# One budget per step for GpSimd's side work, and idle TensorE transposes in all odd steps ahead of the expert slots, in a kernel of top-k attention with a mixture of experts

## The chip, the cores and the metric

The kernel runs on one core of a Trainium2 chip. The metric is the device time of one execution in microseconds (us), the median of several runs. TensorE (PE) multiplies and transposes, VectorE (DVE), ScalarE (ACT) and GpSimd (POOL) work on tiles in SBUF, SyncE (SP) starts most of the transfers. Each engine takes its instructions in the order in which the program wrote them.

## What is computed

```python
scores = scale * np.matmul(q, k.transpose(0, 1, 3, 2))          # 8 batches, 8 heads, 576 x 576, head size 64
kth = np.partition(scores, -32, axis=-1)[..., -32:-31]          # the 32nd largest of each row
scores = np.where(scores >= kth, scores, -1e9)
attn = softmax(scores)                                          # over the row
x = (attn @ v).transpose(0, 2, 1, 3).reshape(4608, 512)
e_idx = np.argmax(x @ w_gate, axis=1)                           # one of 8 experts for each token
for e in range(8):
    mask = e_idx == e
    h = np.maximum(x[mask] @ w1[e], 0.0)                        # 512 -> 1024
    out[mask] = gate_w[mask, None] * eom[mask, e, None] * (h @ w2[e])
```

`gate_w` is the softmax probability of the chosen expert, `eom` a sigmoid of `x @ w_output_gate`. All is float32.

## The kernel before

**Steps.** The attention is cut into 36 tiles of 128 query rows and each tile into 4 head pairs, which gives 144 steps (`for i in range(NSTEP + 4)`, L959). A step writes the work of several head pairs at different stages: VectorE takes the eight largest of each eighth of a row one step ahead (`gmax`, L328) and ranks these candidates of pair i (`rank`, L330 to L339), ScalarE compares its scores with the 24th largest (`below`, L354), GpSimd adds the marks to the scores (`w<-s,marks`, L366, two operations of 128x576), VectorE takes the maxima of that (`window`, L383) and with them, one step later, the 32nd largest and the masked weights (`choose`, `weigh`, L412). TensorE turns the weights of pair i-2 (`flip`, L431: nine transposes in three parts, L438), multiplies those of pairs i-4 and i-3 with the values in every other step (`attend`, L472), and makes the scores of pair i+2 (`scores`, L301), which ScalarE copies (L309).

**Ahead of the slots.** In the first 32 steps (`LONE`, L814) one of the two heads is masked on ScalarE and GpSimd in place of VectorE (`veil`, `unveil`, L418 to L428), so that GpSimd has three 128x576 operations per step. In odd steps `flip` adds 12 transposes of the identity that nobody reads (`IDLE`, L441), but not in steps that carry a routing part (`extra`).

**Routing.** Every fourth step a tile of 128 tokens is done. Two routing parts follow in TensorE's order, `gates` (L502, L493) in an odd step and `rows` (L511, L493) in the next, both written into the same PSUM tile as part 1 of `flip` (`pst`). GpSimd scales the tile's rows in two operations (L515, kind "x") and SyncE writes them to DRAM (`x_rows`). The tiles are collected in 12 groups. After the last tile of a group, GpSimd scatters the tokens' numbers into expert lists (`ids`, L604 and L605, kind "ids") and, for 8 of the groups, computes a table of slots of up to 128 tokens of one expert (`slot_table`, L635: 32 small operations on one partition, kind "table").

**Slots.** From step 33 on a slot takes four steps: its list is loaded (`idt`, issued by ScalarE), GpSimd gathers its 128 rows (`fetch_x`, L754), TensorE turns them (`turn`, L764), multiplies with `w1` in two steps (L775) and with `w2` in two (L790), and GpSimd scatters the result (`put`, L800 and L801, kind "out"). 29 slots start beside the attention, the last in step 145; eleven run in a tail with no attention.

**Order of GpSimd's side work.** `later` puts an operation with an estimated cost into a list in order of due step. Three places in a step take from it: before `below`, kinds "ids" and "out" up to `DMAS` or `MORE`; after `veil`, kind "x" up to `SUMS`; near the step's end, kind "table" up to `TABLES`, in parts of four operations at 0.72. `fetch_x` comes last and its cost counts nowhere, since `spent` is set to zero at each place:

```python
spent[0] = 0.0
run_slow(SUMS, ("x",))
spent[0] = 0.0
...
spent[0] = 0.0
run_slow(TABLES, ("table",))
ahead("x", fetch_x, 2, "id", 1)
```

A group's slots are listed (`queue_slots`) when no "ids" and no "table" waits any more.

Of the kernel before, what the change touches and what calls it, by code (L numbers as in the profile page):

```python
# [10 lines left out]
F32 = mybir.dt.float32  # L11
# [10 lines left out]
ACT = mybir.EngineType.Activation  # L22

P = 128
# [6 lines left out]
USUAL = 9  # L31


SUMS = 1.3
DMAS = 2.2
TABLES = 2.4
MORE = 3.2

NLIST = 12

# [2 lines left out]
def tile_topk_attention_moe(  # L43
# [11 lines left out]
    nc = tc.nc  # L55
# [24 lines left out]
    NID = E * REG + MAXS * P  # L80
# [18 lines left out]
    FIXED = {}  # L99
# [99 lines left out]
    def run(exact, stack):  # L199
# [25 lines left out]
        def later(what, cost, f, due):  # L225
            queued[0] += 1
            slow.append((step[0] + due, queued[0], what, cost, f))
            slow.sort()
# [16 lines left out]
        def waiting(what):  # L245
            return any(x[2] == what for x in slow)
# [184 lines left out]
        def flip(i, part, extra=None, idle=0):  # L431

            pt = EP[i].rearrange("p a s -> p (a s)")
            c0, c1 = ((0, 4), (4, 5), (5, 9))[part]
            n = c1 - c0
            ps = ps_t.tile([P, 4, P], F32, name="pst")
            for c in range(c0, c1):
                nc.tensor.transpose(ps[:, c - c0, :], pt[:, c * P:(c + 1) * P], ident)  # L438
            ev = extra(ps) if extra else None
            for _ in range(idle):  # L440
                nc.tensor.transpose(ps[:, 3, :], ident, ident)  # L441
            x = wk.tile([P, n, P], F32, name=f"pT{n}", bufs=6 if n == 4 else 3)
            PTT.setdefault(i, []).append(x)
            if part == 2:
                del EP[i]

            def copies():
                nc.scalar.activation(x, ps[:, :n, :], AF.Copy)  # L448
                if ev:
                    ev()  # L450
            return copies
# [283 lines left out]
            W.setdefault(s, [None, None])[1] = b  # L735

        def fetch_id(s, g, k, rows):
            eng, queue = ACT, nc.scalar
            if g in FIXED:
                place = slice(FIXED[g][k] * REG, FIXED[g][k] * REG + P)  # L740
            else:
                ov = nc.values_load(SLOT[g][0:1, 1, k:k + 1], engines=[eng], min_val=0, max_val=NID - P,
                                    skip_runtime_bounds_check_because="expert regions and the spare one hold every slot")
                place = bass.ds(ov, P)
            it = mp.tile([P, 4], I32, name="idt", bufs=NLIST)
            queue.dma_start(it, ids[place, :])
            G[s] = [it]

        def fetch_x(s, g, k, rows):
# [171 lines left out]
        def route(g):  # L921
            ops = group_route(g, LGT[g])
            small.extend(ops[:-1])
            if g < NGRP - 1:
                def some(part):
                    for f in part:
                        f()
                if g in FIXED:
                    parts = [settle(FIXED[g])]
                else:  # L930
                    table = slot_table(g, False)
                    parts = [table[x:x + 4] for x in range(0, len(table), 4)]

                def tables():
                    for part in parts:
                        later("table", 0.18 * len(part), lambda part=part: some(part), 1)

                def chosen():
                    order.extend((g, k, (GROUPS[g][-1] + 1) * P) for k in range(EARLY[g]))
                if g in FIXED:  # L940
                    chosen()
                    small.extend([ops[-1], tables])
                else:
                    small.extend([tables, ops[-1], lambda: not waiting("table"), chosen])
                small.append(lambda: not waiting("ids"))
                small.append(lambda: not waiting("table"))
                small.append(lambda: queue_slots(g, EARLY[g], (GROUPS[g][-1] + 1) * P))
            else:
                small.extend(ops[-1:])
# [9 lines left out]
        for i in range(NSTEP + 4):  # L959
# [10 lines left out]
                fill(2)  # L970
                weigh(i - 1)
            spent[0] = 0.0
            run_slow(DMAS if i < LONE else MORE, ("ids", "out"))
            fetch_ids()
            if i < NSTEP:
                below(i)
# [4 lines left out]
            if 2 <= i < NSTEP + 2:  # L981
                early.append(flip(i - 2, 0))
                if i < LONE or not extra:
                    early.append(flip(i - 2, 1, extra, idle=0 if i >= LONE or extra or i % 2 == 0 else IDLE))
            if 4 <= i < LONE and i % 2 == 0:
                late.append(attend(i - 4))
            ahead_of_slot()
# [22 lines left out]
            if 1 <= i <= NSTEP:  # L1010
                veil(i - 1)
            spent[0] = 0.0
            run_slow(SUMS, ("x",))
            spent[0] = 0.0
            if i < NSTEP:
                exps(i)
            for f in late:
# [6 lines left out]
            if i < NSTEP:  # L1024
                window(i, 0)
                window(i, 1)
            spent[0] = 0.0
            run_slow(TABLES, ("table",))
            ahead("x", fetch_x, 2, "id", 1)
            side_use()  # L1030
            fill(3)
            if i < NSTEP:
# [26 lines left out]
        def background():  # L1059
            step[0] += 1  # L1060
            extra = side_start()
            if extra:
                extra(ps_t.tile([P, 4, P], F32, name="pst"))()
                side_use()
            fill(60)
            run_slow(1e9, ("table", "ids", "x", "out"))

        tail[0] = True
        HL = {}
# [149 lines left out]
```

## Time and profile before

| | |
|---|---|
| three runs | 1259.98, 1263.29, 1263.64 us; median 1263.29 |
| the profiled execution | 1265.04 us; its span 1263.3 us |
| busy in the span | TensorE 1163.9 us (92%), VectorE 1066.4 (84%), ScalarE 950.2 (75%), GpSimd 715.0 (57%) |
| chain that ended last | TensorE 38%, VectorE 23%, issue 16%, GpSimd 15%, ScalarE 5% |

The span is some 2 us shorter than the execution's time, because the execution also has a start and an end outside the instructions. A busy share is a mean over the whole span; the first 32 steps, the steps with slots and the tail have different limits and have to be read apart.

### The profile page before, as it was taken

The page shows a single profiled execution, that of the slowest core. Times are in us where ns is not written, and L with a number is a line of the kernel's source. Part 1 is how long each engine was busy: PE and PEld are TensorE (multiplying, and loading weights), DVE is VectorE, ACT ScalarE, POOL GpSimd, SP SyncE. Part 2 cuts the span into 40 slices and gives each one's busy share as a digit, 9 for nine tenths or more (in the row PEclk, how much of TensorE's full clock was granted, in tenths as well). Part 3 has the DMA queues.
Part 4 walks back from the last instruction along what each step waited for, and adds up shares of the span by engine and source line. Part 5 has one row for each costly group of instructions (what it writes and reads, how often), then busy time and mean ns, then how long its engine had stood idle before and what let it go on. Part 6 is the DMA issues. An engine that isn't in the chain of part 4 may idle for free.

```text
span 1263.3 us, 31073 instructions
## 1 busy us (share of the span) xinstructions
PE 1163.9 (92%) x9862; PEld 893.0 (71%) x9862; DVE 1066.4 (84%) x6145; ACT 950.2 (75%) x1892; POOL 715.0 (57%) x1191
## 2 busy tenths in 40 slices
PE   5777777899999999999999999999999999979996
PEld 3555555677777777777776777777777777869995
DVE  6999898899999999998998999989999988344442
ACT  5998898888878887787887878878787877334542
POOL 6666668554546584866566765576755485321110
PEclk7989898899999999999999999999999999989998
DMA  5300136067545448486554655566464444599980
GB/s 138 70 18 27 43 115 254 19 203 249 191 162 159 144 145 304 141 239 226 191 175 173 205 204 192 183 210 210 133 237 169 160 148 172 193 341 353 365 320 21
DMA packets 113734, 227.47 MB, mean 180 GB/s; under 512 B 19206, under 2 KB 37894, under 8 KB 112528
## 3 DMA queue, kind: packets, MB, share of 16 engines
q1 hardware_dynamic: 99712, 205.61, 48.4%
q0 software_dynamic: 7552, 18.96, 4.4%
q10 hardware_dynamic: 6288, 0.74, 0.5%
q8 instruction: 82, 1.34, 0.4%
q14 instruction: 100, 0.82, 0.2%
HBM read 206.68 MB, written 20.69 MB: 180 GB/s over the span
## 4 chain that ended last, share of the span: by engine, by line
PE 38%; DVE 23%; issue 16%; POOL 15%; ACT 5%; ACTq 1%; DMA 1%; POOLq 0%
PE pm L775 9%; PE pm L790 8%; PE po L472 7%; DVE cand L328 7%; PE ps L301 6%; POOL w L366 6%; PE pst L438 6%; DVE v L383 4%; DVE ep L412 4%; DVE cand L339 3%; DVE v L336 3%; POOL ids L605 2%; ACT marks L363 1%; POOL out_dram L801 1%; DVE x L394 1%
## 5 line engine op out<-in xcount | busy, mean ns | idle before, releaser
L366 POOL TENSOR_TENSOR w<-s,marks 128x576 f32<-128x576 f32 x288 | 363.3, 1283 | 256.6 <-DVE ep L412 121.2
L328 DVE MAX8 cand<-s 128x8 f32<-128x72 f32 x2304 | 323.9, 219 | 14.2 <-ACT s L309 14.2
L775 PE MATMUL pm<-xs,w1t 128*128 128x128 f32 x2560 | 297.3, 275 | 0.0
L775 PEld LDWEIGHTS pm<-xs,w1t 128*128 128x128 f32 x2560 | 292.0, 192 | 0.9
L438 PE MATMUL pst<-ident,ep 128*128 128x128 f32 x1296 | 221.7, 287 | 64.9 <-ACT ep L428 46.8
L363 ACT ACTIVATE marks<-s,v 128x576 int8<-128x576 f32 x288 | 220.6, 769 | 67.8 <-DVE v L336 44.9
L383 DVE MAX8 v<-w 128x8 f32<-128x576 f32 x288 | 207.8, 749 | 51.8 <-POOL w L366 51.6
L438 PEld LDWEIGHTS pst<-ident,ep 128*128 128x128 f32 x1296 | 147.9, 143 | 141.3 <-ACT ep L428 55.0
L448 ACT ACTIVATE pT<-pst 128x512 f32<-128x512 f32 (+1 forms) x432 | 200.5, 485 | 32.3 <-PE pst L493 26.9
L790 PE MATMUL pm<-w2t,ht 128*128 128x512 f32 x464 | 208.9, 593 | 0.0
L412 DVE SCALAR_TENSOR_TENSOR ep<-s,kth,ep 128x576 f32<-128x576 f32 x256 | 200.5, 816 | 0.0
L309 ACT ACTIVATE s<-ps 128x1152 f32<-128x1152 f32 (+1 forms) x145 | 163.3, 1127 | 43.2 <-PE ps L301 41.1
L378 ACT ACTIVATE ep<-s,v 128x576 f32<-128x576 f32 x256 | 185.7, 771 | 11.4 <-POOL v L352 11.4
L301 PE MATMUL ps<-kst,qst 64*128 64x288 f32 (+1 forms) x1280 | 184.8, 437 | 5.1 <-ACT s L309 5.1
L472 PEld LDWEIGHTS po<-pT,v 128*64 128x64 f32 x3200 | 168.2, 144 | 25.0 <-issue 24.0
L472 PE MATMUL po<-pT,v 128*64 128x128 f32 (+1 forms) x3200 | 185.3, 275 | 0.1
L790 PEld LDWEIGHTS pm<-w2t,ht 128*128 128x128 f32 x464 | 83.6, 190 | 83.7 <-issue 83.4
L301 PEld LDWEIGHTS ps<-kst,qst 64*128 64x128 f32 (+1 forms) x1280 | 99.5, 180 | 47.3 <-issue 23.8
L336 DVE MAX8 v<-cand 128x8 f32<-128x16 f32 (+2 forms) x864 | 128.7, 189 | 0.0
L801 POOL DMA_INDIRECT out_dram<-y,idt x40 | 48.1, 1203 | 134.4 <-ACT y L797 113.4
L339 DVE MATCH_REPLACE8 cand<-v,cand 128x16 f32<-128x16 f32 (+1 forms) x576 | 95.1, 174 | 0.0
L352 POOL TENSOR_SCALAR v<-v 128x2 f32<-128x2 f32 x144 | 37.1, 258 | 94.6 <-DVE v L336 93.9
(169 smaller groups left out, 1234.6 us busy)
## 6 DMA issues: line engine op xcount, KB each, us to landing
w1t<-in_w_dram SPq DMA_DIRECT2D x40, 2048.0 KB
w2t<-in_w_dram SPq DMA_DIRECT2D x40, 2048.0 KB
x_rows<-xu SPq DMA_DIRECT2D x36, 256.0 KB
qst<-in_qa_dram SPq DMA_DIRECT2D x70, 128.0 KB
v<-in_va_dram SPq DMA_DIRECT2D x8, 1024.0 KB
kst<-in_ka_dram SPq DMA_DIRECT2D x14, 576.0 KB
v<-in_va_dram SPq DMA_DIRECT2D x16, 64.0 KB
ids<-far SPq DMA_DIRECT2D x1, 678.0 KB
```

Source lines behind the costliest of these rows:

```text
L301: nc.tensor.matmul(ps[qs, a, n, :288], Q[t][rows, hp, qs], K[b][rows, hp, cols], start=True, stop=True)
L328: nc.vector.max(out=c[:, 8 * g:8 * g + 8], in_=SC[i, a][:, g * GW:(g + 1) * GW])
L363: nc.scalar.activation(m.bitcast(I8).rearrange("p (s b) -> p s b", b=2)[:, :, 1], s, AF.Sign, bias=vs[:, a, PIVOT - 1:PIVOT], scale=-(1.0 ...
L366: x = nc.gpsimd.tensor_tensor(w, s, m, op=ALU.add)
L378: nc.scalar.activation(EP[i][:, a, :], SC[i, a], AF.Exp, bias=VV[i][0][:, a, 32:33], scale=SCALE)
L383: nc.vector.max(out=VV[i][0][:, a, 24:32], in_=SW[i][0][a])
L412: LAST[0] = nc.vector.scalar_tensor_tensor(e, SC.pop((i, a)), kth_col(i, a), e, op0=ALU.is_ge, op1=ALU.mult, accum_out=SM[t][:, 2 * hp + a ...
L438: nc.tensor.transpose(ps[:, c - c0, :], pt[:, c * P:(c + 1) * P], ident)
L448: nc.scalar.activation(x, ps[:, :n, :], AF.Copy)
L472: nc.tensor.matmul(po[a * 64:(a + 1) * 64, k, qs], lhs, rhs, start=half and not k and not m, stop=(c == 3 and k == 1 and m == len(TT[t]) - 1))
L775: nc.tensor.matmul(ph[:, f - f0, :], w[:, c, f * P:(f + 1) * P], XS[s][:, c, :], start=(c == 0), stop=(c == NC - 1))
L790: nc.tensor.matmul(PY[s], HT[s][:, f, :], w[:, f, :], start=(f == 0), stop=(f == NF - 1))
```

## The change

The three places become two. Before `below` "ids" and "out" go as before, up to 2.6, but up to 1.4 (one of them) while a table waits. After `veil` the gathers go first, then "x", "table" and "done" in their order, all on one budget: 1.3 ahead of the slots, 2.75 with them. A table's operations are put into the list singly at 0.27, and the last six of its 32, which only the next table needs, are a kind of their own ("done") that listing the slots does not wait for. The idle transposes are written into a PSUM tile of their own (`spare`, of the experts' pool) and are no longer left out in steps with a routing part. One variable in `fetch_id` is renamed away.

```diff
--- before.py
+++ after.py
@@ -31,10 +31,10 @@
 USUAL = 9
 
 
-SUMS = 1.3
-DMAS = 2.2
-TABLES = 2.4
-MORE = 3.2
+DMAS = 2.6
+MORE = 1.4
+FEW = 1.3
+MANY = 2.75
 
 NLIST = 12
 
@@ -437,8 +437,9 @@
             for c in range(c0, c1):
                 nc.tensor.transpose(ps[:, c - c0, :], pt[:, c * P:(c + 1) * P], ident)
             ev = extra(ps) if extra else None
+            spare = pools["p"].tile([P, 4, P], F32, name="pm") if idle else None
             for _ in range(idle):
-                nc.tensor.transpose(ps[:, 3, :], ident, ident)
+                nc.tensor.transpose(spare[:, 0, :], ident, ident)
             x = wk.tile([P, n, P], F32, name=f"pT{n}", bufs=6 if n == 4 else 3)
             PTT.setdefault(i, []).append(x)
             if part == 2:
@@ -735,15 +736,14 @@
             W.setdefault(s, [None, None])[1] = b
 
         def fetch_id(s, g, k, rows):
-            eng, queue = ACT, nc.scalar
             if g in FIXED:
                 place = slice(FIXED[g][k] * REG, FIXED[g][k] * REG + P)
             else:
-                ov = nc.values_load(SLOT[g][0:1, 1, k:k + 1], engines=[eng], min_val=0, max_val=NID - P,
+                ov = nc.values_load(SLOT[g][0:1, 1, k:k + 1], engines=[ACT], min_val=0, max_val=NID - P,
                                     skip_runtime_bounds_check_because="expert regions and the spare one hold every slot")
                 place = bass.ds(ov, P)
             it = mp.tile([P, 4], I32, name="idt", bufs=NLIST)
-            queue.dma_start(it, ids[place, :])
+            nc.scalar.dma_start(it, ids[place, :])
             G[s] = [it]
 
         def fetch_x(s, g, k, rows):
@@ -922,18 +922,12 @@
             ops = group_route(g, LGT[g])
             small.extend(ops[:-1])
             if g < NGRP - 1:
-                def some(part):
-                    for f in part:
-                        f()
-                if g in FIXED:
-                    parts = [settle(FIXED[g])]
-                else:
-                    table = slot_table(g, False)
-                    parts = [table[x:x + 4] for x in range(0, len(table), 4)]
+                table = settle(FIXED[g]) if g in FIXED else slot_table(g, False)
+                aside = 0 if g in FIXED else 6
 
                 def tables():
-                    for part in parts:
-                        later("table", 0.18 * len(part), lambda part=part: some(part), 1)
+                    for n, f in enumerate(table):
+                        later("table" if n < len(table) - aside else "done", 0.27, f, 1)
 
                 def chosen():
                     order.extend((g, k, (GROUPS[g][-1] + 1) * P) for k in range(EARLY[g]))
@@ -970,7 +964,7 @@
                 fill(2)
                 weigh(i - 1)
             spent[0] = 0.0
-            run_slow(DMAS if i < LONE else MORE, ("ids", "out"))
+            run_slow(MORE if waiting("table") else DMAS, ("ids", "out"))
             fetch_ids()
             if i < NSTEP:
                 below(i)
@@ -981,7 +975,7 @@
             if 2 <= i < NSTEP + 2:
                 early.append(flip(i - 2, 0))
                 if i < LONE or not extra:
-                    early.append(flip(i - 2, 1, extra, idle=0 if i >= LONE or extra or i % 2 == 0 else IDLE))
+                    early.append(flip(i - 2, 1, extra, idle=0 if i >= LONE or i % 2 == 0 else IDLE))
             if 4 <= i < LONE and i % 2 == 0:
                 late.append(attend(i - 4))
             ahead_of_slot()
@@ -1010,8 +1004,8 @@
             if 1 <= i <= NSTEP:
                 veil(i - 1)
             spent[0] = 0.0
-            run_slow(SUMS, ("x",))
-            spent[0] = 0.0
+            ahead("x", fetch_x, 2, "id", 1)
+            run_slow(FEW if i < LONE else MANY, ("x", "table", "done"))
             if i < NSTEP:
                 exps(i)
             for f in late:
@@ -1024,9 +1018,6 @@
             if i < NSTEP:
                 window(i, 0)
                 window(i, 1)
-            spent[0] = 0.0
-            run_slow(TABLES, ("table",))
-            ahead("x", fetch_x, 2, "id", 1)
             side_use()
             fill(3)
             if i < NSTEP:
@@ -1063,7 +1054,7 @@
                 extra(ps_t.tile([P, 4, P], F32, name="pst"))()
                 side_use()
             fill(60)
-            run_slow(1e9, ("table", "ids", "x", "out"))
+            run_slow(1e9, ("table", "done", "ids", "x", "out"))
 
         tail[0] = True
         HL = {}
```

GpSimd's order in step 89 before, in the middle of a group's table (`v` and `near` are the step's first operations, `spacer` stands ahead of each scatter, `sl_` and `first_row` are the table's):

```order
L352 TENSOR_SCALAR v_10131<-v_10131 128x2
L400 COPY near<-v_10012 128x4
L604 MEMSET spacer 1x1
L605 DMA ids<-entry,posi 43392x4
L800 MEMSET spacer 1x1
L801 DMA out_dram<-y,idt 4608x512
L366 TENSOR_TENSOR w<-s,marks_80 128x576
L366 TENSOR_TENSOR w<-s,marks_81 128x576
L515 TENSOR_TENSOR xu<-xu,r 128x256 x2
L675 TENSOR_TENSOR sl_jump<-first_row 1x8
L676 TENSOR_SCALAR sl_jump<-sl_jump 1x8
L679 TENSOR_TENSOR sl_way<-sl_past,sl_jump 1x24
```

The same step after the change:

```order
L352 TENSOR_SCALAR v_10241<-v_10241 128x2
L400 COPY near<-v_10111 128x4
L605 MEMSET spacer 1x1
L606 DMA ids<-entry,posi 43392x4
L366 TENSOR_TENSOR w<-s,marks_80 128x576
L366 TENSOR_TENSOR w<-s,marks_81 128x576
L754 DMA xg_129<-x_rows,idt 128x512
L669 TENSOR_SCALAR first_row<-pad_d 1x8
L670 TENSOR_TENSOR first_row<-first_row,done 1x8
L676 TENSOR_TENSOR sl_jump<-first_row 1x8
L677 TENSOR_SCALAR sl_jump<-sl_jump 1x8
L680 TENSOR_TENSOR sl_way<-sl_past,sl_jump 1x24
```

The scatter of the result and the two scalings have left the step (they stand in step 91), the gather has come up from the step's end to behind the second `w`, and six of the table's operations follow it where twelve stood. Before, the table was written in steps 88, 89 and 90 as 12, 12 and 8 operations; now it is 10, 6, 10 and, in step 91, the last 6. The other seven tables are spread in the same way.

TensorE's order from the scores of step 6 into step 7 before (`xT` is the attention's result, `lt` the gates' logits; the five `pst<-ident,ep` are parts 0 and 1 of `flip`, the four its part 2):

```order
L301 MATMUL ps<-kst,qst 128x288 x4
L438 MATMUL pst<-ident,ep 128x128 x5
L502 MATMUL pst<-xT,wg 32x128 x4
L493 MATMUL pst<-ident,xT 128x128 x2
L438 MATMUL pst<-ident,ep 128x128 x4
```

And after the change:

```order
L301 MATMUL ps<-kst,qst 128x288 x4
L438 MATMUL pst<-ident,ep 128x128 x5
L503 MATMUL pst<-xT,wg 32x128 x4
L494 MATMUL pst<-ident,xT 128x128 x2
L442 MATMUL pm<-ident 128x128 x12
L438 MATMUL pst<-ident,ep 128x128 x4
```

The 12 idle transposes stand between the gates' products and the last part of `flip`, and write `pm`. This is so in steps 7, 11, 15, 19, 23, 27 and 31; the other odd steps had them already. The steps in which each slot's products start are the same before and after.

## Rows read from the trace of the kernel before

**Rows 1.** Busy time by stage: start:end, length, engines' busy us, granted clock, DMA share, GB/s.

```profile
0.00:237.20 237.20, 167.70 (x1443) 121.72 (x1445) 210.73 (x1348) 202.44 (x426) 157.30 (x232) 0.86 0.31 90
237.20:1069.40 832.20, 823.53 (x7201) 617.69 (x7200) 777.35 (x4691) 673.29 (x1383) 518.98 (x910) 1.00 0.56 187
1069.40:1263.30 193.90, 172.66 (x1221) 153.62 (x1220) 78.32 (x110) 74.47 (x85) 38.71 (x50) 0.95 0.72 259
```

**Rows 2.** VectorE's waits in the slots' stage: total us, times, longest us.

```profile
DVE v L383 <- POOL w L366: 38.7, 49, 2.3
```

**Rows 3.** TensorE's waits in the same stage.

```profile
PE pst L502 <- ACT xT L474: 4.9, 6, 1.4
PE pst L764 <- DMA xg<-x_rows,idt: 1.6, 1, 1.6
```

**Rows 4.** Windows of steps 45 to 48, 101 to 104, and 89, 90, 91.

```profile
327.10:356.50 29.40, 29.40 (x248) 22.14 (x247) 27.66 (x164) 24.20 (x50) 15.37 (x21) 1.00 0.50 173
756.90:784.50 27.60, 27.60 (x235) 20.98 (x234) 27.35 (x166) 22.89 (x48) 15.36 (x22) 1.00 0.55 191
656.10:666.00 9.90, 9.90 (x115) 8.78 (x112) 7.39 (x45) 7.81 (x15) 8.93 (x19) 1.00 0.67 239
666.00:675.60 9.60, 9.33 (x88) 7.39 (x88) 6.80 (x41) 5.76 (x12) 8.29 (x22) 1.00 0.71 254
675.60:682.40 6.80, 5.41 (x31) 2.74 (x30) 6.80 (x44) 4.69 (x13) 3.88 (x9) 1.00 0.21 68
```

**Rows 5.** GpSimd's timeline, steps 88 and 89: start us, us, instruction, idle before.

```profile
652.81 2.52 POOL L366 TENSOR_TENSOR w<-s,marks 128x576 f32<-128x576 f32 x2
655.29 0.20 POOL L652 TENSOR_TENSOR sl_cnt<-base,carry 1x8 f32<-1x8 f32 x1
...
658.53 0.60 POOL L669 TENSOR_TENSOR first_row<-first_row,done 1x8 f32<-1x8 f32 x1
...
660.24 1.09 POOL L605 DMA_INDIRECT ids<-entry,posi  x1 [0.17 <-issue]
...
665.11 1.21 POOL L515 TENSOR_TENSOR xu<-xu,r 128x256 f32<-128x256 f32 x2
...
670.81 1.13 POOL L754 DMA_INDIRECT xg<-x_rows,idt  x1 [0.61 <-DVE cand L328]
```

**Rows 6.** Windows of steps 5-6, 7, 10, 13, 20-21, 10-25, 31-32.

```profile
43.00:55.30 12.30, 9.15 (x89) 6.83 (x88) 12.13 (x80) 11.94 (x25) 8.16 (x11) 1.00 0.55 123
55.30:61.50 6.20, 3.86 (x26) 2.46 (x27) 6.17 (x43) 6.15 (x14) 4.11 (x6) 0.76 0.00 1
77.50:83.50 6.00, 4.60 (x57) 3.43 (x54) 5.96 (x40) 5.82 (x13) 4.03 (x6) 1.00 0.01 1
95.90:104.30 8.40, 6.64 (x51) 4.66 (x47) 6.84 (x43) 7.10 (x15) 5.21 (x8) 0.99 0.20 63
143.20:159.30 16.10, 13.41 (x138) 10.08 (x135) 13.04 (x82) 12.87 (x28) 9.27 (x13) 0.77 0.36 86
77.50:186.30 108.80, 80.45 (x807) 58.98 (x804) 101.11 (x644) 99.12 (x213) 69.89 (x89) 0.91 0.15 42
222.60:237.20 14.60, 9.48 (x53) 5.91 (x53) 13.46 (x90) 13.42 (x29) 10.49 (x14) 0.73 0.12 29
```

**Rows 7.** TensorE's timeline, steps 5, 10, 11 and 12.

```profile
45.24 1.47 PE L441 MATMUL pst<-ident 128*128 128x128 f32 x12
...
79.39 2.40 PE L472 MATMUL po<-pT,v 128*64 128x128 f32 x40
...
87.53 0.66 PE L438 MATMUL pst<-ident,ep 128*128 128x128 f32 x4 [0.94 <-ACT pT L448]
...
92.31 4.07 PE L472 MATMUL po<-pT,v 128*64 128x128 f32 x40
```

**Rows 8.** VectorE's timeline, end of step 12 and start of 13: reading the gates.

```profile
95.79 0.27 DVE L528 TENSOR_TENSOR tl<-pst,r 128x128 f32<-128x128 f32 x1
96.10 0.37 DVE L530 TENSOR_REDUCE lg<-tl 128x16 f32<-128x128 f32 x1
```

## Prediction

> **What bounds the kernel now.** I read the windows of the three stages first, then who waits in each, then single steps.
>
> By stage [rows 1] the first 32 steps take 237.2 us, the 112 steps with slots 832.2 us, the tail 193.9 us. The reader is to see that different engines are full: ahead of the slots VectorE (210.7 of 237.2) and ScalarE (202.4), TensorE with 167.7 at a mean granted clock of 0.86; in the slots' stage TensorE, 823.5 of 832.2, at full clock. The change touches nothing in the tail, and each slot starts in the same step as before, so the tail is costed at nothing; what covers it is its own weights' transfers (DMA share 0.72).
>
> *Slots' stage.* VectorE waits 38.7 us there for GpSimd's `w` [rows 2], and this is the number one would like to win. TensorE's own waits are the counter-check: 4.9 and 1.6 us [rows 3], together with smaller ones 832.2 - 823.5 = 8.7 us in which it is not busy. Steps 45 to 48 take 29.4 us with TensorE busy through all of them and GpSimd busy for 15.4; steps 101 to 104, with GpSimd no busier, take 27.6 [rows 4]. The difference is backlog. In steps 89 and 90 GpSimd is the last one (8.9 of 9.9 us, 8.3 of 9.6, where a step otherwise takes about 7, by 27.6 or 29.4 for four), and TensorE still works on through 9.9 of 9.9 and 9.3 of 9.6: it uses the stall to finish what lay before it. Only step 91, where it has caught up, shows it idle, 6.8 - 5.4 = 1.4 us. After such a stall VectorE sets a pace of 27.6 per four steps until TensorE is behind again, then TensorE sets 29.4. So over a cycle TensorE bounds this stage, and a GpSimd stall costs only what TensorE idles after it.
>
> *Ahead of the slots.* Step 10 takes 6.0 us at clock 1.00, step 13 takes 8.4, steps 20 and 21 together 16.1 at a mean clock of 0.77 [rows 6]. In step 12, at the lower of the two levels (1.2 GHz in place of 2.4), the 40 products of `attend` took 4.07 us, against 2.40 in step 10 [rows 7]; the scores behind them came late, then ScalarE's copy and marks, GpSimd's `w`, and with them VectorE in step 13. What TensorE did before a fall: steps 5 and 6, of which 5 has idle transposes, run at 1.00; step 7, an odd step without them, is at 0.76 over its length and the fall lies in it [rows 6]. There are eight such falls, the first in step 7 and the last in step 31 (both windows in [rows 6]): four in odd steps with a routing part and no idle transposes (7, 19, 27, 31), four in even steps (12, 16, 24, 30), none in an odd step with them.
>
> **The change part by part.**
>
> 1. *Idle transposes in steps 7, 11, 15, 19, 23, 27, 31.* Each adds 12 transposes, 1.47 us in step 5. They stand where TensorE waits 0.94 us for ScalarE in step 11 [rows 7], so at most 1.47 - 0.94 = 0.53 us per step goes behind the wait, and the scores come that much later. The lower bound of their cost is nothing (ScalarE is still at other work when the scores are done), the upper 7 x 0.53 = 3.7 us; I take 0.2 each, 1.4 in all. If the cover were gone, all 1.47 would count, 10.3 us. What they may give: undisturbed, a cycle of four steps takes 4 x 6.1 us (6.0 in step 10, 6.2 in step 7 [rows 6]), and the step after `rows` some 0.65 more, in which VectorE reads the gates (0.27 and 0.37 [rows 8]): 25.05. Steps 10 to 25 took 108.8 [rows 6], which is 108.8 - 4 x 25.05 = 8.6 us above it. The fall in step 7 resembles that in 19: steps 20 and 21 together take 16.1 against 6.1 + 6.75, so 3.2 more. Steps 31 and 32 take 14.6, but with VectorE busy for 13.5 of them [rows 6], so I count 1.0 there. Upper bound 8.6 + 3.2 + 1.0 = 12.8 us. The lower bound is no gain. The falls in even steps stand open: three of them (12, 16, 24) cost about 8.4 - 6.75 = 1.65 each, and no idle transposes are written into even steps. But those in the odd step before push the scores and the next transposes by up to 0.53 us into the gap in which the fall came. I take half of these 4.9 as won: 12.8 - 2.4 - 1.4 = **9.0 us**.
>
> 2. *GpSimd's budget.* No work is removed: scatters (pitch about 1.4 us with the memset ahead), gathers (1.13), scalings (1.21 for two) and table operations, 11 from 655.29 to 658.53, 0.30 us each [rows 5]. It is dealt out anew. Step 88 gets one scatter, `w` (2.52), 0.44 for the two small copies and 10 table operations: 1.4 + 2.52 + 0.44 + 3.0 = 7.4. Step 89: one scatter, the gather with its gap of some 0.3, six operations: 1.4 + 2.96 + 1.4 + 1.8 = 7.6. Step 90 is as 88, step 91 has scalings, scatter and the last six: 1.2 + 1.4 + 2.96 + 1.8 = 7.4. The sum is 29.8 us over four steps, beside TensorE's 29.4: GpSimd is then just level with TensorE in place of 9.9 and 9.6 us in two steps and idle around them. What is late next is TensorE, at its own pace. So the gain is bounded by its 8.7 idle us; the lower bound is nothing, since with 29.8 against 29.4 GpSimd may still be last at some steps. I take 6.0, nearer the upper end, because a lag of 0.4 us per group is small beside a backlog that lasted from step 91 to step 104. "ids" and "out" are delayed by a step or two at most; what waits for them (listing, list loads on ScalarE, turning the rows) has spare steps, since slots start as before.
>
> 3. *Moved without price:* the gather ahead of the scalings (its list was loaded at the step's start, and `w` runs for 2.52 us in between); idle transposes into another PSUM tile, which is free until step 33; the last six table operations, which only the next table reads; the budget 1.3 ahead of the slots, which still takes two scalings.
>
> **Sum.** 9.0 + 6.0 = 15.0 us. Against the profiled execution, 1265.0 - 15.0 = 1250.0; this execution lies 1.7 us above the median of the three runs, so I put the new median at 1263.3 - 15.0 = **1248.3 us**. A measurement of this kernel tells about 0.3% (3.8 us) from no change.
>
> **The rivals.**
>
> *VectorE's waits come back whole.* Were VectorE the bound of the slots' stage, 38.7 us [rows 2] would go and the time would be about 1225. Against it speaks TensorE, busy through the stalls. Chance 0.03.
>
> *Only one half works.* If the clock still falls in the even steps, or falls in others because the steps have moved against the times at which the clock changes, 3 us remain of part 1: 1263.3 - 9 = 1254. If GpSimd, full for four steps in place of two, leaves TensorE idle as before, part 2 is nothing: also 1254. Against the first: even steps without a routing part, such as step 10 at 1.00 [rows 6], never fell. Chance of one or the other 0.28.
>
> *Neither works, or one is eaten up,* 1260 to 1266: 0.09. That the change does not do what it says is excluded by the order: the transposes and the dealt-out table stand there.
>
> *Slower: the idle transposes do not hold the clock and are in the way.* TensorE has no slack in the first stage if the scores' end is what ScalarE waits for. Then each of the seven steps is 1.47 us longer, 10.3 us, while falls come as before: 1263.3 + 10.3 - 6.0 = 1267.6. It decides from the point where the scores end later than ScalarE's work before their copy. For it: ScalarE is busy in 202.4 of 237.2 us [rows 1], so any delay of it is passed on. Against it: odd steps with the transposes take 12.3 us together with the even step after them [rows 6], no more than two even steps. Chance 0.06. The Trainium skill (TensorE: Matmul & The Clock Gate, Part 4: PE-mode transpose) says that full clock "doesn't engage for transpose-mode (it doesn't count as PE-busy the same way)". By that rule the new transposes could hold nothing and this rival would be the forecast, 1267.6. The trace speaks against it: steps 5 and 6 hold 1.00 with them, step 7 falls without them.
>
> **How the numbers follow.** Both halves work: 0.54, with 1240 to 1254 as its own range (both upper bounds, 12.8 + 8.7 = 21.5 us, and the 1.7 us by which executions differ; 9 us at the least). One half: 0.28. VectorE's waits: 0.03. Neither: 0.09. Slower: 0.06. The range from 1240 to 1260 leaves out the last, the first rival and most of "neither". Faster than 1259.5 is 0.54 + 0.28 + 0.03 and a little of "neither", 0.86; within 0.3% 0.08; slower 0.06.
>
> **What would show it.** Steps 8, 9, 13, 17, 20 and 21 at 6 to 7 us, the granted clock of the first stage above 0.95 (0.86 now), 12 transposes in step 11 with little or no wait behind them. In the slots' stage: steps 89 and 90 at 7 to 8 us, VectorE's wait for `w` well under 38.7, but TensorE's busy time unchanged near 823 and the stage shorter only by TensorE's idle time. The forecast is wrong if the stage shrinks by much more than 8.7 us (then TensorE was not its bound), or if falls of the clock remain in even steps, or if the steps with idle transposes are longer than their neighbours.

## The result, and the profile after

The changed kernel takes 1244.24 us in the median of four runs (1243.55 to 1246.53), the kernel before 1261.65 beside it (1259.98 to 1263.64): a ratio of 0.9865, 95% interval 0.9841 to 0.9888, 17.4 us faster. The forecast was 1248.3 in a range from 1240 to 1260. The profiled execution took 1243.92, its span 1242.1.

The same three stages after the change (start:end, length, busy us of PE, PEld, DVE, ACT, POOL with the number of instructions, granted clock, DMA share, GB/s), to be held against [rows 1]:

```profile
0.00:226.10 226.10, 161.00 (x1529) 120.14 (x1531) 209.59 (x1348) 201.31 (x427) 156.97 (x232) 0.93 0.33 95
226.10:1050.30 824.20, 820.71 (x7200) 617.00 (x7196) 785.22 (x4691) 672.52 (x1382) 512.56 (x910) 1.00 0.56 189
1050.30:1242.10 191.80, 171.94 (x1221) 153.15 (x1221) 77.65 (x110) 74.56 (x85) 38.51 (x50) 0.96 0.72 262
```

The first stage is 237.2 - 226.1 = 11.1 us shorter at a clock of 0.93 in place of 0.86, the slots' stage 832.2 - 824.2 = 8.0, the tail 193.9 - 191.8 = 2.1. These add to 21.2, more than the medians' 17.4, since the profiled execution of before lies 3.4 us above its median (1265.04 against 1261.65).

**Ahead of the slots**, windows of steps 7, 10, 13, 20 with 21, 10 to 25, 31 with 32 [rows 6]:

```profile
54.90:61.10 6.20, 4.80 (x43) 3.60 (x42) 6.17 (x43) 6.12 (x14) 4.10 (x6) 1.00 0.00 1
74.00:80.10 6.10, 4.70 (x57) 3.52 (x56) 6.07 (x42) 5.85 (x13) 4.12 (x6) 1.00 0.01 1
92.40:99.10 6.70, 4.95 (x38) 3.44 (x35) 6.62 (x43) 6.38 (x14) 5.18 (x8) 1.00 0.25 80
136.50:149.50 13.00, 9.61 (x133) 7.37 (x130) 12.72 (x81) 12.53 (x28) 9.27 (x13) 1.00 0.25 68
74.00:175.30 101.30, 76.20 (x855) 56.69 (x853) 100.27 (x646) 98.67 (x213) 69.95 (x89) 1.00 0.15 41
211.70:226.10 14.40, 9.46 (x65) 6.78 (x66) 13.44 (x90) 13.60 (x30) 10.48 (x14) 0.85 0.13 30
```

Step 13 takes 6.7 us in place of 8.4, steps 20 and 21 13.0 in place of 16.1, and the 16 steps from 10 to 25 take 101.3 in place of 108.8. From step 7 to 25 the clock stays at the upper level; three falls are left, in steps 26, 30 and 32. (The granted clock of 0.93 also holds the stretch of 17.1 us at the lower level that stands at the execution's start, as in the kernel before.) TensorE's timeline in step 11, where the new transposes stand [rows 7]:

```profile
82.67 0.44 PE L494 MATMUL pst<-ident,xT 128*128 128x128 f32 x2
82.95 1.47 PE L442 MATMUL pm<-ident 128*128 128x128 f32 x12
84.26 0.60 PE L438 MATMUL pst<-ident,ep 128*128 128x128 f32 x4
84.79 1.24 PE L301 MATMUL ps<-kst,qst 64*128 64x288 f32 x8
```

The wait of 0.94 us is gone and the idle transposes take its place; the last part of `flip` follows without a gap. Counted from the step's start the scores come 4.7 us into it, 0.1 later than before.

**With slots**, first VectorE's wait for GpSimd and TensorE's own waits [rows 2, 3]:

```profile
DVE v L383 <- POOL w L366: 23.0, 41, 1.8
```

```profile
PE pst L503 <- ACT xT L475: 1.4, 2, 0.8
PE pst L764 <- DMA xg<-x_rows,idt: 0.9, 1, 0.9
PE pst L438 <- ACT pT L449: 0.6, 1, 0.6
```

then the windows of steps 45 to 48, 101 to 104, and 89, 90, 91 [rows 4]:

```profile
315.90:345.30 29.40, 29.40 (x249) 22.14 (x247) 27.81 (x165) 24.20 (x50) 14.81 (x21) 1.00 0.50 174
733.00:760.60 27.60, 27.60 (x225) 20.77 (x223) 27.55 (x165) 22.95 (x48) 14.82 (x21) 1.00 0.49 179
642.10:650.00 7.90, 7.90 (x97) 7.39 (x97) 7.27 (x43) 6.26 (x14) 7.04 (x14) 1.00 0.68 252
650.00:658.30 8.30, 8.30 (x95) 7.12 (x89) 6.93 (x43) 7.19 (x13) 7.60 (x18) 1.00 0.12 34
658.30:666.50 8.20, 7.57 (x51) 4.12 (x45) 8.10 (x44) 4.27 (x12) 6.79 (x16) 1.00 0.48 140
```

VectorE waits 15.7 us less for `w`, but the stage is only 8.0 shorter. TensorE is idle for 824.2 - 820.7 = 3.5 us, where it was 8.7. Steps 45 to 48, which TensorE paced, are as long as before to the tenth. Steps 89 to 91 take 7.9, 8.3 and 8.2 us in place of 9.9, 9.6 and 6.8: the group's work is dealt out evenly, and TensorE works on through two of the three. Not every table comes out so: three of the eight are dealt out as this one, in 10, 6, 10 and 6 operations, the other five in 10, 10, 10 and 2. In steps 115 and 139, where two of these five end, two scalings and two scatters stand as well, and the step takes 9.3 us, with TensorE busy throughout; step 115:

```profile
834.20:843.50 9.30, 9.30 (x81) 5.73 (x77) 7.01 (x44) 6.38 (x14) 8.39 (x18) 1.00 0.08 30
```

GpSimd's timeline in step 89 shows how little lies between its two large pairs now [rows 5]:

```profile
646.72 2.53 POOL L366 TENSOR_TENSOR w<-s,marks 128x576 f32<-128x576 f32 x2
649.41 1.05 POOL L754 DMA_INDIRECT xg<-x_rows,idt  x1 [0.16 <-PE pst L438]
650.49 0.25 POOL L669 TENSOR_SCALAR first_row<-pad_d 1x8 f32<-1x8 f32 x1
...
652.62 0.64 POOL L685 TENSOR_TENSOR sl_past<-sl_past 1x12 f32<-1x12 f32 x1
...
653.80 1.11 POOL L606 DMA_INDIRECT ids<-entry,posi  x1 [0.17 <-issue]
654.95 2.52 POOL L366 TENSOR_TENSOR w<-s,marks 128x576 f32<-128x576 f32 x2
```

From `w` to `w` it is 8.2 us; before, step 88 needed 9.8 and step 89 9.7.

### The profile page after: what moved, and what is told of

Same layout as the page of the kernel before. It is cut to its first block, busy times and chain, and to the rows that moved or that the text cites. A ratio compares the mean times of both kernels' runs of the same rounds, so it can differ in the third digit from the quotient of the medians.

```text
span 1242.1 us, 31234 instructions
## 1 busy us (share of the span) xinstructions
PE 1153.7 (93%) x9946; PEld 890.3 (72%) x9946; DVE 1072.5 (86%) x6145; ACT 948.4 (76%) x1892; POOL 708.0 (57%) x1191
## 4 chain that ended last, share of the span: by engine, by line
PE 59%; issue 14%; DVE 14%; POOL 8%; ACT 2%; DMA 1%; ACTq 1%; POOLq 0%
PE pm L775 14%; PE pm L790 13%; PE po L473 10%; PE ps L301 9%; PE pst L438 9%; DVE cand L328 4%; POOL w L366 3%; DVE v L383 3%; DVE ep L412 2%; DVE cand L339 2%; DVE v L336 2%; PE pst L494 1%; ACT marks L363 1%; PE pst L764 1%; POOL out_dram L801 1%
## 5 line engine op out<-in xcount | busy, mean ns | idle before, releaser
L438 PE MATMUL pst<-ident,ep 128*128 128x128 f32 x1296 | 217.5, 283 | 59.7 <-ACT ep L428 49.7
L301 PE MATMUL ps<-kst,qst 64*128 64x288 f32 (+1 forms) x1280 | 181.2, 431 | 5.1 <-ACT s L309 5.1
L473 PEld LDWEIGHTS po<-pT,v 128*64 128x64 f32 x3200 | 161.9, 139 | 24.6 <-issue 23.7
L473 PE MATMUL po<-pT,v 128*64 128x128 f32 (+1 forms) x3200 | 178.8, 268 | 0.1
```

Source lines behind the costliest of these rows:

```text
L301: nc.tensor.matmul(ps[qs, a, n, :288], Q[t][rows, hp, qs], K[b][rows, hp, cols], start=True, stop=True)
L473: nc.tensor.matmul(po[a * 64:(a + 1) * 64, k, qs], lhs, rhs, start=half and not k and not m, stop=(c == 3 and k == 1 and m == len(TT[t]) - 1))
```

## The experiments

All times are medians, each compared with runs of the kernel before on the same chip. Stages are cut where VectorE ends step 32 and step 143, so that the first has 33 steps and the second 111.

**1. The idle transposes alone.** The kernel before with

```diff
+            spare = pools["p"].tile([P, 4, P], F32, name="pm") if idle else None
             for _ in range(idle):
-                nc.tensor.transpose(ps[:, 3, :], ident, ident)
+                nc.tensor.transpose(spare[:, 0, :], ident, ident)
...
-    early.append(flip(i - 2, 1, extra, idle=0 if i >= LONE or extra or i % 2 == 0 else IDLE))
+    early.append(flip(i - 2, 1, extra, idle=0 if i >= LONE or i % 2 == 0 else IDLE))
```

> The kernel before with the idle transposes of the change alone (all odd steps ahead of the slots, in a PSUM tile of their own); GpSimd's budgets as before. Theory (two separate gains: the clock ahead of the slots, TensorE's idle time with the slots): the first stage gets 10 to 11 us shorter, as in the changed kernel (237.2 to about 227), its granted clock rises from 0.86 to about 0.93, the slots' stage stays at 832 within 2; time about 1251. Rival A (transposes do not hold the clock, and what shortened the first stage was GpSimd's budget): no change, 1261 to 1265. Rival B (the gain of the whole needs both parts): under 4 us, 1258 to 1262.

Measured: 1251.39 against 1261.25, ratio 0.992 (0.9905 to 0.9935), 9.9 us. Windows of the first and the second stage:

```profile
0.00:227.10 227.10, 160.90 (x1533) 119.68 (x1533) 209.80 (x1349) 201.35 (x427) 157.10 (x232) 0.94 0.33 94
227.10:1057.80 830.70, 822.33 (x7196) 617.17 (x7194) 777.02 (x4689) 671.93 (x1382) 517.55 (x910) 1.00 0.56 187
```

The first stage is as in the changed kernel, the second nearly as in the one before, with TensorE idle for 8.4 us. Both rivals fall.

**2. The budget alone.** The changed kernel with `flip` and its call as before (the lines of experiment 1, reversed).

> The changed kernel with the idle transposes as before (none in odd steps with a routing part); GpSimd's one budget alone. Theory: the first stage stays at about 237 with a granted clock near 0.86, the slots' stage gets 6 to 8 us shorter (832 to about 825) because TensorE's idle time there falls from 8.7 to some 3 us; time 1253 to 1256. Rival A (the budget did all): about 1244. Rival B (the budget does nothing by itself): 1261.

Measured: 1253.61 against 1261.25, ratio 0.9936 (0.992 to 0.9952), 7.6 us. Windows of its two stages:

```profile
0.00:232.80 232.80, 160.69 (x1443) 115.16 (x1445) 210.41 (x1349) 201.72 (x426) 156.88 (x232) 0.89 0.32 92
232.80:1056.70 823.90, 820.44 (x7200) 616.88 (x7198) 785.25 (x4689) 672.36 (x1383) 513.70 (x910) 1.00 0.56 189
```

The slots' stage is 823.9, as in the changed kernel. The first stage was expected at 237 and took 232.8; its clock still falls six times, in steps 8, 11, 16, 23, 27 and 31, in part other steps than before. Of the 4.4 us 3.1 lie in steps 20 and 21, because no fall came in step 19 here. Steps 28 to 31 gain half a microsecond in the changed kernel (30.0 against 30.4). The rest is one execution's pattern of falls, and I don't count it to the budget: over the whole span the mean granted clock of its six executions is 0.969, as in the 17 of the kernel before beside them, against 0.983 in experiment 1.

**3. The change unaltered.** No edit.

> The changed kernel unaltered, so that its two parts are compared with it on the same chip. Theory of two separate gains: 1244, and its gain over the kernel before is the sum of the gains of the two parts within 3 us. Rival (the parts overlap): the sum of the parts' gains is above the whole by more than 3 us.

Measured: 1244.26 against 1261.25, ratio 0.9864 (0.9847 to 0.9881), 17.0 us. The parts alone gave 9.9 and 7.6, in sum 17.5: the gains are separate.

**4. No idle transposes.** The changed kernel with

```diff
-        IDLE = 12
+        IDLE = 0
```

> The changed kernel with no idle transposes at all. Theory (the transposes hold the clock): the clock falls in odd steps too, the first stage takes 240 to 255 us at a granted clock under 0.85, time 1258 to 1275. Rival (transposes do not count for the clock, as a page's rule has it): the first stage stays at 226 or gets shorter by some tenths, time 1242 to 1245.

Measured: 1263.03 against 1261.25, ratio 1.001 (0.9998 to 1.0021). First stage:

```profile
0.00:244.20 244.20, 167.78 (x1351) 114.98 (x1353) 212.31 (x1348) 201.98 (x426) 156.88 (x232) 0.82 0.30 88
```

The clock falls 16 times from step 3 to step 32, in 14 of the 15 odd steps and in steps 16 and 32, and the stage takes 244.2 us, 18.1 more than with them. The Trainium skill (TensorE: Matmul & The Clock Gate, Part 4: PE-mode transpose) says that full clock does not engage for transposes. The trace does not agree for these float32 transposes of 128x128: with 12 of them in every odd step no profile has a fall from step 4 to step 23, and without them nearly every odd step has one.

**5 to 7. The same 0.75 us on each of three engines.** In the 46 steps with slots that have no routing part in part 1 of `flip`, the changed kernel gets one addition (the comments give the experiment; the conditions that pick the steps are left out here):

```diff
+            for _ in range(more):        # 5: in flip, more=7
+                nc.tensor.transpose(ps[:, 3, :], ident, ident)
...
+                    nc.vector.max(out=wk.tile([P, 8], F32, name="xtra", bufs=2), in_=SW[i][0][1])   # 6: behind window
...
+                xtra = wk.tile([P, 352], F32, name="xtra", bufs=1)      # 7: behind the side work
+                nc.gpsimd.memset(xtra, 0.0)
+                nc.gpsimd.memset(xtra, 0.0)
```

> The changed kernel with 7 more idle transposes in the 46 steps with slots that have no routing part in part 1 of flip: 7 x 0.109 = 0.76 us of TensorE each, 35 us in all. Theory (TensorE bounds the slots' stage over a cycle): nearly all of it shows, 30 to 36 us, the slots' stage 854 to 860, time 1274 to 1280. Rival (VectorE or GpSimd bounds it and TensorE only looks busy): under 10 us, time under 1254.

> The changed kernel with one more maximum over 128x576 on VectorE, 0.75 us, in the same 46 steps, 34.5 us in all. Theory (VectorE has some slack to TensorE: 27.6 against 29.4 per four steps without routing, less with it): the 1.5 such operations per four steps (1.1 us) just fit, 5 to 15 us show, time 1249 to 1259. Rival (VectorE is the bound): nearly all of it, 1274 to 1280.

> The changed kernel with two more memsets of 128x352 on GpSimd, 0.75 us together, behind the side work of the same 46 steps, 34.5 us in all. Theory (GpSimd has slack in most steps, and its lag in the steps with tables is covered by TensorE's backlog): 0 to 6 us show, time 1244 to 1250. Rival (GpSimd is the bound now, full in the steps with tables): 15 us or more, over 1259.

Measured against 1260.98 of the kernel before and against 1244.2 of the change, which was not run on this chip: 1273.83 with more on TensorE (ratio to before 1.0105, 1.0082 to 1.0128), 1250.72 on VectorE (0.9917, 0.989 to 0.9943), 1250.87 on GpSimd (0.9914, 0.9895 to 0.9933). Of some 35 us added 29.6 show on TensorE, 6.5 on VectorE, 6.6 on GpSimd, each give or take some 3 us. The slots' stage of the three, in this order:

```profile
226.50:1076.80 850.30, 849.77 (x7495) 648.65 (x7491) 788.35 (x4689) 674.38 (x1378) 514.57 (x910) 1.00 0.55 183
```

```profile
226.50:1055.20 828.70, 821.31 (x7204) 617.12 (x7201) 810.37 (x4736) 673.47 (x1383) 505.15 (x910) 1.00 0.56 188
```

```profile
228.20:1057.70 829.50, 821.81 (x7200) 617.15 (x7196) 782.45 (x4690) 671.54 (x1381) 553.07 (x1002) 1.00 0.56 188
```

With more on TensorE it is idle for 0.5 us of the stage; with more on the others its busy time stays at 821 to 822 and its idle time rises from 3.5 to 7.4 and 7.7. TensorE is the bound; the other two took some 28 of the 35 us without a loss. Two sizes were missed. With more on TensorE the slots' stage was expected at 854 to 860 and took 850.3, 26.1 us more than without; the other 3.5 us stand in the tail (195.3 against 191.8). That GpSimd paid 6.6 us is a little above the 0 to 6 that were expected.

**8. Two scatters while a table waits.** The changed kernel with

```diff
-            run_slow(MORE if waiting("table") else DMAS, ("ids", "out"))
+            run_slow(DMAS, ("ids", "out"))
```

> The changed kernel with up to two scatters per step also while a table waits (2.6 in place of 1.4); the rest of the one budget as it is. Theory (only TensorE's idle time after a stall counts, and stalls of under 2 us are covered): steps 88 to 90 get 1 to 2 us longer, TensorE's idle time with slots rises from 3.4 to 4 to 6 us, time 1245 to 1248. Rival (the limit on the scatters is what gave the gain): TensorE's idle time is back at 8 to 9 us, time 1250 to 1253.

Measured: 1243.73 against 1260.98, ratio 0.9865 (0.9846 to 0.9885); the slots' stage:

```profile
226.90:1049.50 822.60, 819.51 (x7199) 616.46 (x7198) 785.80 (x4689) 672.42 (x1382) 511.68 (x910) 1.00 0.57 189
```

TensorE's idle time is 3.1 us. Step 89 got 1.3 us longer, as expected, but step 90 got 1.4 shorter. Neither the 1 to 4 us that I expected nor the rival's loss came: the limit on the scatters by itself is worth nothing that can be measured.

**9. Budgets of their own again.** The changed kernel with

```diff
             ahead("x", fetch_x, 2, "id", 1)
-            run_slow(FEW if i < LONE else MANY, ("x", "table", "done"))
+            spent[0] = 0.0
+            run_slow(FEW if i < LONE else SUMS, ("x",))
+            spent[0] = 0.0
+            run_slow(FEW if i < LONE else 3.3, ("table", "done"))
```

where `SUMS` is 1.3 again.

> The changed kernel with the one budget behind veil taken apart again: gathers are not counted, two scalings and 12 table operations each have a budget of their own (the two heaviest steps get a scatter, the gather, both scalings and 12 table operations, some 10.6 us of GpSimd by the rows of before); the limit of one scatter while a table waits stays. Theory (the one budget is what gave the gain with slots, since without the scatters' limit it stayed): TensorE's idle time with slots is 6 to 9 us, time 1248 to 1252. Rival (either of the two limits is enough): idle 3 to 4 us, 1243 to 1246.

Measured: 1265.34 against 1262.02, ratio 1.002 (1.0007 to 1.0033), 3 us slower than the kernel before and 21 us over the change. The slots' stage and, within it, two stretches at the lower clock:

```profile
227.10:1067.40 840.30, 825.59 (x7198) 619.33 (x7196) 783.48 (x4689) 672.11 (x1380) 515.92 (x910) 0.99 0.55 185
671.60:675.00 3.40, 3.40 (x13) 1.99 (x12) 3.26 (x22) 2.96 (x7) 0.46 (x3) 0.50 0.01 2
859.30:862.70 3.40, 3.20 (x12) 1.90 (x12) 3.21 (x14) 2.97 (x7) 2.69 (x3) 0.50 1.03 366
```

TensorE's longest waits in the stage (total us, times, longest us):

```profile
PE pst L503 <- ACT xT L475: 6.2, 4, 3.6
PE pst L438 <- ACT pT L449: 5.5, 2, 3.2
```

Without the one budget the gain is gone, as the theory had it, but 21 us go where 4 to 8 were expected. In the rest this is not the kernel before: the gather still stands ahead of the scalings and the table, and one scatter goes per step while a table waits. So the run shows that beside these the one budget is needed; the gather's new place was not undone alone. TensorE is idle for 840.3 - 825.6 = 14.7 us, and at its three longest waits (3.6 us in step 91, 2.3 in step 116, 3.2 in step 140) its clock fell, each time for 3.4 us (the third at 1043.6). In the kernel before its longest wait with slots was 1.6 us [rows 3], and the clock did not fall there. The stage is 840.3 - 824.2 = 16.1 us longer: 11.2 of idle time and 4.9 of busy time, which is about half of the three stretches. Another 3.6 us of the 21 stand in the tail (195.4 against 191.8).

**10. Waits filled in every step.** The changed kernel with

```diff
                 early.append(flip(i - 2, 0))
+                if 3 <= i <= LONE:
+                    gap = pools["p"].tile([P, 4, P], F32, name="pm")
+                    for _ in range(IDLE):
+                        nc.tensor.transpose(gap[:, 0, :], ident, ident)
```

> The changed kernel with 12 idle transposes (1.3 us) also between parts 0 and 1 of flip in steps 3 to 32, even ones too, where TensorE waits 1.4 us or more for ScalarE's weights. Theory (the clock still falls in steps 24 to 32 because TensorE waits there; what lies inside the wait costs nothing): no fall from step 3 to 32, the first stage 222 to 225 us (226.1 now), time 1240 to 1243. Rival (the 1.3 us push the weights' turns back by a little in each step, and 30 steps pay 0.1 to 0.3 each): the first stage 228 to 232, time 1246 to 1250.

Measured: 1243.78 against 1262.02, ratio 0.9859 (0.9842 to 0.9876). Window of its first stage:

```profile
0.00:225.20 225.20, 196.63 (x1903) 155.51 (x1905) 209.61 (x1349) 201.02 (x427) 157.11 (x232) 0.96 0.34 95
```

No fall from step 4 to the tail in this execution, TensorE busy for 196.6 us of the stage in place of 161.0, and the stage only 0.9 us shorter. 30 times 1.3 us inside a wait cost nothing that can be measured. The stage lies just above the 222 to 225 that I expected, the time just above 1240 to 1243: the last falls were worth about 1 us, which is within what runs differ by.

**11. No early flush.** The changed kernel with the scalings written early only where rows are missing, and one scatter per step until "done" is empty:

```diff
-            flush("x")
+            if rows_done[0] < rows:
+                flush("x")
...
-            run_slow(MORE if waiting("table") else DMAS, ("ids", "out"))
+            run_slow(MORE if waiting("table") or waiting("done") else DMAS, ("ids", "out"))
```

> The changed kernel with one scatter per step until the last six table operations are done too, and with the scalings no longer all written ahead of the step's two large operations when a group's slots are listed (only where rows are still missing). Theory (TensorE bounds the stage; only 3.4 us of its idle time are left): steps 91, 99, 115 and 139 get up to 2 us shorter, the time by no more than 2: 1242 to 1245. Rival (GpSimd's lag in these steps is on the path): 6 us or more, under 1239.

Measured: 1245.23 against 1262.02, ratio 0.9862 (0.9844 to 0.988): no difference from the change, although steps 115 and 139 went from 9.3 to 8.0 us. Steps 116 and 140 behind them went from 6.7 to 7.5 and 8.1, so most of what one step gained the next one took. Step 91, also expected to get shorter, stayed at 8.2.

**12. Experiments 8 and 10 together.**

> The changed kernel with the filled gaps of gap_filled and the two scatters of two_scatters together. Theory (both are within what TensorE's pace hides; only the last falls of the clock, some 1 us, are still to be had): 1242 to 1244, not to be told from the change. Rival (the two add up beyond that): under 1240.

Measured: 1241.98 against 1263.17, ratio 0.9838 (0.982 to 0.9856), the lowest of all, with an interval that overlaps that of the change (0.9847 to 0.9881): not shown to be faster than it. Windows of its two stages:

```profile
0.00:225.10 225.10, 197.62 (x1891) 157.13 (x1893) 209.71 (x1348) 201.26 (x427) 157.34 (x232) 0.95 0.33 95
225.10:1049.40 824.30, 820.27 (x7198) 616.61 (x7197) 786.54 (x4690) 673.02 (x1382) 514.98 (x910) 1.00 0.56 189
```

Here the clock fell in steps 30 and 32, though the waits were filled as in experiment 10: filling them does not keep the clock up in every execution.

## Why the prediction was right

**Bounds.** That TensorE, over a cycle, bounds the slots' stage held: experiments 5 to 7 show it directly (29.6, 6.5 and 6.6 us of 35). That VectorE and ScalarE bound the first stage was not tested by adding work to them; experiment 10 shows that TensorE does not, since 35.6 us more of its work made the stage no longer. Of the tempting 38.7 us of VectorE's wait 15.7 went, for 8.0 us, and the rival that took them whole fell.

**Part 1, idle transposes: 9.0 forecast, 9.9 measured alone.** Of the bounds, steps 10 to 25 gave 7.5 us of 8.6. The fall in step 7, priced at 3.2 after steps 20 and 21, gave 3.1, in steps 8 and 9 (windows before and after):

```profile
61.50:77.50 16.00, 13.30 (x99) 9.86 (x95) 13.06 (x82) 12.90 (x28) 9.29 (x13) 0.77 0.11 34
```

```profile
61.10:74.00 12.90, 9.52 (x93) 7.16 (x91) 12.76 (x83) 12.58 (x28) 9.30 (x13) 1.00 0.13 42
```

Steps 31 and 32 gave 0.2 of 1.0. Two terms taken off these bounds were mis-sized, in the same direction. *Half of the even steps' falls were to remain.* None did before step 24, in any profile with the transposes in all odd steps. Experiment 4 explains it: without idle transposes every odd step brings a fall (that of step 15 came in step 16). So of the eight falls before the change, those in steps 12, 16 and 24 belonged to the odd steps 11, 15 and 23 ahead of them, which had no idle transposes either; all seven such steps had their fall, in the step itself or in the next. Experiment 2 bears this out: with the same transposes as before, steps 11 and 23 had the fall themselves there, and that of step 7 came in step 8. My split into "odd" and "even" falls was by where the clock fell, not by what TensorE had done before. *The price of 0.2 us per step* was 0.1 in step 11, and nothing in any step that can be seen in its length. What remained are falls from step 24 on. The one in step 30 stands behind a GpSimd stall (step 29, with two scatters, takes 9.4 us before and still 8.7 after), and TensorE's wait behind it is as long as before; its timeline in step 30, before and after:

```profile
217.99 0.33 PE L438 MATMUL pst<-ident,ep 128*128 128x128 f32 x1 [3.57 <-ACT ep L428]
```

```profile
205.94 0.48 PE L438 MATMUL pst<-ident,ep 128*128 128x128 f32 x1 [3.58 <-ACT ep L428]
```

Step 30 has no routing part, so the prediction's sentence that even steps without one never fell was wrong there. Why the others from step 24 on remain was not tried.

**The slower rival** needed transposes that don't count for the clock and scores that come 1.47 us later. Both are shown wrong, by experiment 4 and by the timeline of step 11. One row against it was read too kindly: the 12.3 us of steps 5 and 6 are a little more than two steps of 6.0, not "no more".

**Part 2, the budget: 6.0 forecast, 7.6 measured alone.** Steps 88 to 91 take 31.3 us (33.2 before), not the 29.8 of the working, so GpSimd's lag behind TensorE's 29.4 is 1.9 us and not 0.4; the backlog covered most of that too. TensorE's idle time fell from 8.7 to 3.5 us, 5.2, near the 6.0; another 2.8 us came out of its busy time (823.5 to 820.7), which I had taken as fixed. Of this 1.2 us lie in the gates' products, one of the places where TensorE waits for ScalarE [rows 3]: these 224 products show 14.3 us before and in experiment 1, 13.1 after and 13.0 in experiment 2. Some of the stalls' cost may thus stand in shown lengths of operations in place of idle time; no run separates it. Experiments 8 and 9 say what matters in the edit: the one budget for gathers, scalings and table together is needed, the limit on scatters is not. Whether the gather's new place or the kind "done" does anything by itself stays open.

**The prediction's own signs.** The steps that it named went to 6.2 to 6.9 us, and step 11 lost its wait, as it said. Three signs went against it. The clock of the first stage is 0.93, not above 0.95 (0.96 in experiment 10, which has no fall after the start). Falls remain in even steps (26, 30 and 32), which it had called a sign of being wrong. And with slots not only TensorE's idle time went. The falls that remain left the forecast standing because only 1.0 us had been counted on there: steps 26 to 32 take 50.9 us before and 50.8 after.

**The tail** was costed at nothing, and is 2.1 us shorter in the profiled pair. Some 50 us into it stands a stretch at the lower clock; windows of it before and after:

```profile
1120.10:1130.30 10.20, 4.80 (x14) 3.94 (x15) 1.22 (x1) 2.40 (x2) 1.10 (x3) 0.50 1.03 387
```

```profile
1102.30:1109.20 6.90, 2.99 (x9) 2.57 (x10) 0.00 (x0) 1.84 (x2) 0.00 (x0) 0.51 1.03 394
```

The shorter stretch stands in both profiles of the changed kernel, in experiments 8 and 12 and, without the budget, in experiment 1; the longer one stands in experiments 10 and 11, which have all edits of the change. Over all profiles the tail takes 190.8 to 191.9 us with the shorter one and 192.3 to 195.5 with the longer one. So the change by itself does not decide it, and I don't count the 2.1 us to it.

**The sum.** Without the tail the profiled pair gives 19.1 us, the medians 17.4, the forecast 15.0: the parts, as measured alone, were too careful by 0.9 and 1.6 us. The median lies 4.1 us under the 1248.3 forecast, and 1.6 of these are the base, since the kernel before measured 1261.65 beside the change and not 1263.3.

## What to carry to other kernels

Ask of a wait what the engine that bounds the stage does meanwhile: as long as it works off a backlog the wait is free, so count that engine's idle time, not the wait (here 38.7 us of wait stood against 8.7 of idle time, and 8.0 were won). Spread side work so that no step exceeds the backlog, with one limit over everything the engine does in it, since several small limits add up in the same step. Idle matrix work that lay wholly inside an existing wait cost nothing here that could be measured, and kept the clock up in all but a few steps.

## What was not expected

- Over the backlog a stall costs more than its idle time: in experiment 9 three falls of TensorE's clock in the slots' stage took 4.9 us on top of 11.2 us of idle time. Before the change steps of nearly the same length (9.9 and 9.6 us, against up to 10.4) brought no fall there. What differs is TensorE's single wait behind them: 2.3 to 3.6 us at the falls, 1.6 at most before the change.
- The same program's clock falls in different steps in different executions: the two profiles of the changed kernel have them in steps 26, 30 and 32, and in 24, 28 and 32; experiments 10 and 12, with the same transposes, have none and two. What decides it was not tried.
